# Another queue for the row stores of five segments, and a four-and-two split of the left products, in a recurrent memory transformer with a dense GELU block

## The chip, the cores and the metric

The kernel runs on one core of a Trainium2 chip. The core has five engines with an instruction stream each: TensorE (PE, with its weight loads shown as PEld), VectorE (DVE), ScalarE (ACT), GpSimd (POOL) and SyncE (SP). SP, ACT and POOL issue the transfers (DMA) of this kernel. The metric is the device time of one execution in microseconds (us); lower is better. The time before is the median of three runs.

## The reference

The output is the sum of three things over the same input x of 2048 rows by 1024: x itself, a dense block, and a recurrent attention. Cut to what matters:

```python
xn = layernorm(x)
B = gelu(xn @ w1 + b1) @ w2 + b2                    # 1024 -> 3584 -> 1024
mem = mem0                                          # 8 rows
for s in range(64):                                 # segments of 32 rows
    h = concat([mem, xn[32*s:32*s+32]])             # 40 rows
    q, k, v = h @ Wq, h @ Wk, h @ Wv                # 32 heads of 128
    p = softmax(where(mask, q @ k.T / sqrt(128), -1e9))
    o = (p @ v) @ Wo                                # 40 rows by 1024
    mem, out[s] = o[:8], o[8:]
return x + out + B
```

mask lets every row see the 8 memory rows and the rows up to itself. The loop is a chain: the memory rows of a segment are the first rows of the next one's h. All data is bf16, sums are kept in f32.

## The kernel before

**First stage, up to about 428 us.** Layernorm, the dense block and the residual sum x + B, which is written to DRAM as R_n. The normalised rows go to DRAM too, in the layout that the loop wants (hr_d, hrL_d). While this stage ends, the attention weights are fetched.

**The loop (from L725) over 64 segments, s.** A segment has 64 weight units of 128 x 2048, in the order K0, Q0, K1, Q1, V0, V1 (eight units each, `half_pass`, L767; the digit is the half of the heads) and O (sixteen units, loop at L1104). 46 units live in SBUF. 18 are streamed again from DRAM in every segment into six slots; two of these are kept in PSUM and copied by DVE (L246), one is kept in part. `PLACED` says which units are streamed. As soon as PE has used a streamed unit, `unit_done` (L709) lets SP start the transfer of a later one into its slot, and lets POOL issue one or two entries of a list `small`.

**Main and left rows.** Of each 32 rows a segment handles 24 together with its 8 memory rows (hT, 32 rows, kept in hr_home). The other 8 rows of four segments are gathered into a set of 32 left rows (hL), since nothing in the recurrence waits for them; each half pass of K, Q and V does the left rows once in a group of four segments. i4 is s modulo 4. Where a half pass does both, each weight unit is used twice, by four matmuls each (`product`, L743).

**The turn of the memory rows.** At the end of a segment the sums of O are put together (ACT L1124 where i4 is 1, else DVE L1128), turned by PE (`put_mem`, L295) and copied by DVE into the next hT (L305). Only then can the next K0 begin. Around this stand left products of one of the next segment's half passes, made ahead of time on weights that live in SBUF: up to LEAD = 6, half of them before `put_mem` and the rest behind it:

```python
led.update(next=(w, u, new_acc(), ahead, order), made=0)
lead_products(LEAD // 2)
put_mem(o_sb, nxt["hT"], mixed[:, 224:288], 4 // nw)
if led:
    lead_products(LEAD)
```

They are made at 60 of the 63 turns; in the last group of four segments no next left rows exist.

**Rows out.** The residual rows of a segment are loaded into res_home, which is hr_home[:, 256:512] (for s below 5 by ACT at the start of O, L1075). DVE adds the sums of O to them in place (L1148), and four transfers store 24 rows by 256 columns each to the output (L1182, POOL). Where i4 is 1, the rows go to a DRAM tile first (L1154) and from there to the output by entries of `small` (L1179). The next segment writes the probabilities pdB over res_home[:, 0:128] in `sums(0)` (L915), so that has to wait until the stores have read the rows.

**POOL in the first segments.** For s from 1 to 4, `turn_R` (L438, L467) adds copies of the last residual rows, DRAM to DRAM, to `small`; POOL issues them in order with its other work. `moved_values` (L1097) is a copy of left values on POOL where i4 is 3.

**Order on an engine.** Each engine takes its instructions in the order in which the program lists them. `at` in a segment maps a product's number to functions that are listed behind it: `scores` (PE), `sums` (PE, ACT, DVE), `values` (PE, ACT, DVE), `attend`. PSUM has three accumulator banks (`new_acc`, `let_go`), so a half pass can start only when an earlier one's bank was evicted (`rows_out`, L800).

Of the kernel before, what the change touches and what calls it, by code (L numbers as in the profile page):

```python
# [18 lines left out]
S = 2048  # L19
# [29 lines left out]
SCRATCH = 384  # L49
SMALL = 3712  # L50
LEAD = 6
LATER = 3
LAG = 3
STREAM_BUFS = 6
# [18 lines left out]


ORDER = pass_order()
PLACED = "S..S...." "S...S..." "S....S.." ".S.....S" "....S..." "S..S..S." "...S..S." "S..S..SS"
IS_STREAMED = {unit: PLACED[n] == "S" for n, unit in enumerate(ORDER)}
assert PLACED.count("S") == STREAMED
# [11 lines left out]
def kernel(  # L90
# [142 lines left out]
            fetch(res_tiles[unit], unit)  # L233


    streams = [unit for _ in range(NSEG) for unit in ORDER if IS_STREAMED[unit]]
# [418 lines left out]
    with tc.tile_pool(name="late", bufs=1) as late, \  # L655
# [37 lines left out]
        def unit_tile(unit):  # L693
            nonlocal used
            if IS_STREAMED[unit]:
                place_in_stream[unit] = used
                used += 1
                return stream_tiles.pop(used - 1)[:, :]
            return res_tiles[unit]
# [16 lines left out]
                    if small:  # L716
                        small.popleft()()

        O_UNITS = ORDER[48:]

        hT, hL = nxt["hT"], nxt["hL"]
        kL, VL = [None] * 2, [None] * 2
        led = {}
# [1 line left out]
        for s in range(NSEG):  # L725
# [6 lines left out]


            more = g + 1 < NGRP
            left_k = [first or (i4 == 3 and more), i4 == 0]
            left_q = [first or (i4 == 1 and more), first or (i4 == 2 and more)]
            left_v = [i4 == 0, first or (i4 == 3 and more)]
# [29 lines left out]
            def half_pass(w, u, left, at):  # L767


                ps = new_acc()  # L770
                psL, ahead, order = None, [], list(range(KT))
                if left and led and led["next"][:2] == (w, u):
                    psL, ahead, order = led["next"][2:]
                    assert led["made"] == len(ahead)
                    led.clear()
                elif left:
                    psL = new_acc()
                lag = LAG if first else 0
                tiles = {}
                for n in range(KT + lag):  # L780
                    if n < KT:
                        tiles[n] = unit_tile((w, n, u))
                        product(w, n, tiles[n], hT, ps, range(KT))
                    i = n - lag
                    if i < 0:
                        continue
                    t = tiles.pop(i)
# [6 lines left out]
                    for fn in at.get(i, ()):  # L794
                        fn()
                return ps, psL

# [231 lines left out]
            turn_q(psQ)  # L1029
            if left_q[0] and not first:  # L1030
                turn_qL(psQL, 0)
            psK1, psK1L = half_pass("K", 1, left_k[1], {7: [lambda: scores(0)]})
            exps(0, None if first else lambda: q_left(1))
            st["kT", 1] = nat_home
            rows_out(psK1, nat_home, nc.scalar.copy)
# [1 line left out]
                0: [lambda: nc.vector.transpose(out=nat_home, in_=nat_home)],  # L1037
            }
            if not first:
                at[4] = [lambda: sums(0)]  # L1040
            if left_q[1] and not first:
                at[0].insert(0, lambda: keep_q(1))
            if left_k[1]:
                at[1] = [lambda: turn_kL(psK1L, 1)]
            elif left_k[0]:
                at[1] = [lambda: turn_kL(psKL, 0)]
            psQ1, psQ1L = half_pass("Q", 1, left_q[1], at)
            if first:
                turn_qL(psQ1L, 1)
# [13 lines left out]
                st["V", 0] = values_out(psV, v_home, nc.scalar.copy)  # L1063
                exps(1)

            at = {0: [attend]}
            if left_v[1]:
                at.update({3: [lambda: values(0, (0,))], 5: [lambda: values(0, (1,)), lambda: sums(1)]})
            else:
                at.update({4: [lambda: values(0, (0, 1))], 6: [lambda: sums(1)]})  # L1070

            def load_res():
                st["res"] = res_home
# [22 lines left out]
                VL[1] = late.tile([P, 512], BF16, name="VL1")  # L1096
                nc.gpsimd.tensor_copy(out=VL[1].rearrange("p (h t) -> p h t", t=SEG), in_=ahead_v)  # L1097

            at = {5: [lambda: values(1, (0, 1))]}
            if apart:  # L1100
                at[6] = [moved_values]
# [17 lines left out]
            if not final:  # L1119
                o_sb = outM  # L1120
                no = 16 if left_o else 8
                o = psX[:, 0:32 * no].rearrange("p (h e) -> p h e", e=32)
                if left_o:
                    nc.scalar.copy(out=o_sb[:, 0:no, :], in_=o)  # L1124
                else:
                    o = psX[:, 0:256].rearrange("p (h e) -> p h e", e=16)
                    flat = o_sb.rearrange("p h e -> p (h e)")[:, 0:256].rearrange("p (h e) -> p h e", e=16)
                    nc.vector.tensor_tensor(out=flat, in0=o, in1=st["folded"], op=ALU.add)  # L1128
# [31 lines left out]
            if final:  # L1160
                engines = [nc.sync, nc.scalar]
                n = 0
                for w, r in enumerate(tiles):
                    for b in range(2):
                        cs = slice(256 * (2 * b + w), 256 * (2 * b + w) + 256)
                        pieces = [(rows, slice(64 * b + m0, 64 * b + m0 + NX))]
                        for sl, row in left_rows:
                            p0 = 64 * b + NL * sl
                            pieces.append((slice(row, row + NL), slice(p0, p0 + NL)))
                        for o, i in pieces:  # L1170
                            engines[n % 2].dma_start(out=out_flat[o, cs], in_=r[i, :])
                            n += 1
            elif left_o:
                pairs = [(out_flat[rows, :], outL_d[og, m0:m0 + NX, :])]
                pairs += [
                    (out_flat[row:row + NL, :], outL_d[og, NL * sl:NL * sl + NL, :]) for sl, row in left_rows
                ]
                for o, r in pairs:
                    small.append(lambda o=o, r=r: nc.gpsimd.dma_start(out=o, in_=r))  # L1179
            else:  # L1180
                for j in range(4):
                    nc.gpsimd.dma_start(out=out_flat[rows, 256 * j:256 * j + 256], in_=res[32 * j:32 * j + NX, :])  # L1182
            if not final:
                hT = nxt["hT"]
        while small:
# [34 lines left out]
```

## Time and profile before

| what | value |
|---|---|
| median of three runs | 1843.01 us (1841.55 to 1844.73) |
| the profiled execution | 1840.11 us, of which 1838.4 us between its first and last instruction (the span) |
| PE busy over the span | 1725.6 us, 94% |
| DVE, ACT, POOL busy | 960.6, 668.6, 276.5 us |
| read from and written to HBM | 577.63 MB and 28.97 MB |
| mean granted TensorE clock | 0.995 |

How to read the lines: a row of the timeline has the start in us, the length in us, the engine, the line of the kernel, the operation, the tiles as out<-in, the count, and in brackets how long the engine had been idle and what ended that. A row of the chain of waits has start, length and what the end of the program hung on in that stretch. A row of windows gives the stretch, its length, the busy time of each engine, the granted clock, the DMA engines' busy share and the rate. A row of one line's instructions gives the shortest, median and longest in ns, then the first and last start in us. POOLq, ACTq and SPq are the sequencers of these engines. Matmul ends are modelled and matmuls overlap, so distances between starts say more than lengths.

### The profile page before, as it was taken

Reading aid. Unit: us, or ns where it says so; the run is one execution under the profiler, and the core shown is the slowest. Engines: PE = TensorE matmul, PEld = TensorE weight load, DVE = VectorE, ACT = ScalarE, POOL = GpSimd, SP = SyncE. Lnnn points to the kernel's source line nnn. Section 1 sums busy time; section 2 is a strip of 40 time slices with the busy share of each in tenths; the row PEclk is TensorE's granted clock in tenths of the full one; section 3 lists DMA queues with packets and bytes.
Section 4 is the critical chain, followed back from the end, with each engine's and each line's share of the span. In section 5 each row is a group of like instructions: output and inputs, shape, how many; then the busy total and the mean of one; then the engine's idle time right before and its main releaser. Section 6 shows DMA issues by size and latency. Waiting matters only on the chain.

```text
span 1838.4 us, 71529 instructions
## 1 busy us (share of the span) xinstructions
PE 1725.6 (94%) x31187; PEld 874.2 (48%) x31207; DVE 960.6 (52%) x2443; ACT 668.6 (36%) x1572; POOL 276.5 (15%) x542
## 2 busy tenths in 40 slices
PE   8999999998979999999999899999999999999997
PEld 4444444444444444444444444444545444455443
DVE  7657483705445545455454555545555554545544
ACT  6334251602323333333333333333333343333333
POOL 0000001400341111111121111111111111111111
PEclk9999999999999999999999999999999999999999
DMA  9921212769989999999999999999999999999997
GB/s 289 322 80 46 53 45 58 258 211 362 397 323 381 379 380 374 376 386 370 374 388 362 377 365 393 376 379 375 383 381 392 378 385 368 374 390 390 370 379 305
DMA packets 230599, 596.28 MB, mean 324 GB/s; under 512 B 46539, under 2 KB 86043, under 8 KB 230284
## 3 DMA queue, kind: packets, MB, share of 16 engines
q1 hardware_dynamic: 207028, 571.28, 83.1%
q0 software_dynamic: 16384, 16.64, 2.8%
q8 instruction: 244, 4.00, 0.8%
q10 hardware_dynamic: 6872, 3.78, 0.7%
q14 instruction: 71, 0.58, 0.1%
HBM read 577.63 MB, written 28.97 MB: 330 GB/s over the span
## 4 chain that ended last, share of the span: by engine, by line
PE 66%; DMA 25%; issue 4%; DVE 3%; ACT 2%; POOL 1%; DVEq 0%; ACTq 0%; SPq 0%; POOLq 0%
PE acc L749 30%; PE ps L478 10%; DMA u<-Wc_V 10%; PE acc L984 10%; PE ps L599 8%; DMA u<-Wc_O 6%; DMA u<-Wc_Q 5%; PE ps L632 2%; DMA u<-Wc_K 2%; PE acc L930 2%; DVE d_oL L1005 1%; DVE u L246 1%; DMA hr_home<-hr_d 1%; PE pT L632 1%; DVE q_all L1128 1%
## 5 line engine op out<-in xcount | busy, mean ns | idle before, releaser
L749 PE MATMUL acc<-u,hr_home 128*32 128x512 bf16 x11520 | 791.3, 380 | 40.0 <-DMA u<-Wc_V 18.6
L749 PEld LDWEIGHTS <-hr_home 128*32 128x32 bf16 x12288 | 329.1, 96 | 352.7 <-issue 56.8
L749 PE MATMUL acc<-u,hrL 128*32 128x512 bf16 x2880 | 248.3, 381 | 2.3 <-issue 2.2
L246 DVE TENSOR_SCALAR u<-kept 128x512 uint32<-128x512 uint32 x254 | 163.6, 686 | 70.3 <-PE acc L984 42.1
L478 PE MATMUL ps<-u 128*128 128x512 bf16 (+1 forms) x920 | 195.7, 375 | 2.0 <-ACT u L398 2.0
L800 ACT CAST d_oL<-acc 128x512 bf16<-128x512 f32 x143 | 81.9, 585 | 274.7 <-PE acc L749 274.7
L599 PE MATMUL ps<-u 128*128 128x512 bf16 x657 | 146.2, 379 | 0.8
L984 PE MATMUL acc<-u,q_all 128*32 128x256 bf16 (+1 forms) x2096 | 126.5, 301 | 16.4 <-DMA u<-Wc_O 12.7
L478 PEld LDWEIGHTS <-u 128*128 128x128 bf16 x920 | 90.5, 99 | 105.5 <-issue 2.4
L984 PE MATMUL acc<-u,d_oL 128*32 128x512 bf16 x1944 | 134.3, 383 | 4.6 <-DMA u<-Wc_O 2.0
L1182 POOL DMA_DIRECT2D out_dram<-hr_home x188 | 96.2, 512 | 260.6 <-DVE hr_home L1148 247.8
L814 DVE STREAM_TRANSPOSE q_all<-q_all 128x512 bf16<-128x512 bf16 x128 | 90.7, 708 | 75.4 <-ACT q_all L800 75.3
L984 PEld LDWEIGHTS <-q_all 128*32 128x32 bf16 x3381 | 102.2, 96 | 55.4 <-issue 24.2
L804 ACT CAST q_all<-acc 128x512 bf16<-128x512 f32 x128 | 75.2, 588 | 145.0 <-PE mixed L864 141.0
L911 DVE TENSOR_TENSOR pd_main<-pr_all,mixed 128x320 bf16<-128x320 bf16 x128 | 62.4, 488 | 122.3 <-ACT mixed L902 122.3
L268 POOL DMA_DIRECT2D hr_home<-hr_d x58 | 32.8, 565 | 594.4 <-PE acc L749 594.4
L800 ACT CAST q_all<-acc 128x512 bf16<-128x512 f32 x128 | 75.2, 587 | 98.0 <-PE acc L749 97.8
L749 PEld LDWEIGHTS <-hrL 128*32 128x32 bf16 x3072 | 82.9, 96 | 52.3 <-issue 4.4
L599 PEld LDWEIGHTS <-u 128*128 128x128 bf16 x672 | 65.3, 98 | 77.3 <-DVE g_u L560 0.4
L984 PEld LDWEIGHTS <-d_oL 128*32 128x32 bf16 x2592 | 68.1, 97 | 62.1 <-issue 15.3
L902 ACT ACTIVATE mixed<-mixed,small_consts 128x160 f32<-128x160 f32 x256 | 94.3, 368 | 8.4
L552 ACT ACTIVATE g_xb<-ps,b1col 128x512 bf16<-128x512 f32 x112 | 76.8, 685 | 55.5 <-PE ps L478 54.7
(139 smaller groups left out, 2092.7 us busy)
## 6 DMA issues: line engine op xcount, KB each, us to landing
u<-Wc_K SPq DMA_DIRECT2D x256, 512.0 KB
u<-Wc_V SPq DMA_DIRECT2D x256, 512.0 KB
u<-Wc_O SPq DMA_DIRECT2D x256, 512.0 KB
u<-Wc_Q SPq DMA_DIRECT2D x192, 512.0 KB
u<-in_B_w_dram SPq DMA_DIRECT2D x28, 512.0 KB
hr_home<-hr_d POOLq DMA_DIRECT2D x58, 128.0 KB, 5.3
u<-in_A_Wq_dram SPq DMA_DIRECT2D x13, 512.0 KB
u<-in_A_Wv_dram SPq DMA_DIRECT2D x12, 512.0 KB
```

The source lines that it names most:

```text
L246: nc.vector.tensor_single_scalar(out=out, in_=in_, scalar=0, op=ALU.bitwise_or)
L478: nc.tensor.matmul(ps[:, SEG * s0:SEG * s1].rearrange("p (s t) -> p s t", t=SEG), lhsT=w1_sb[fb // 2][:, kt, (fb % 2) * P:(fb % 2 + 1) * P ...
L552: nc.scalar.activation(out=xb[:, :], in_=ps[:, :], func=ACT.Identity, bias=b1col[:, fb:fb + 1], scale=1.0)
L599: nc.tensor.matmul(ps[:, :], lhsT=gts[fc // 4][:, fc % 4, t * P:(t + 1) * P], rhs=w2_sb[fc // 2][:, fc % 2, cs], start=(fc == 0), stop=(fc ...
L749: nc.tensor.matmul(o, lhsT=lhs[:, i, :], rhs=m, start=(i == seq[0]), stop=(i == seq[-1]), tile_position=(0, 32 * j),)
L800: cp(out=out, in_=ps.rearrange("p (h e) -> p h e", e=32))
L804: cp(out=t[:, :], in_=ps[:, :])
L814: nc.vector.transpose(out=home, in_=home)
L902: nc.scalar.activation(out=mixed[:, 160 * b:160 * b + 160], in_=mixed[:, 0:160], func=ACT.Exp, scale=-1.0, bias=off[:, b:b + 1],)
L911: nc.vector.tensor_tensor(out=pdA.rearrange("p c b q -> p b c q"), in0=prA[:, None, :, :].to_broadcast([P, 2, 4, 40]), in1=dd, op=ALU.mult,)
L984: nc.tensor.matmul(acc[r0:r0 + rows, c:c + wide], lhsT=lhsT, skip_group_check=True, rhs=cols, start=start, stop=stop, tile_position=(0, r0),)
L1182: nc.gpsimd.dma_start(out=out_flat[rows, 256 * j:256 * j + 256], in_=res[32 * j:32 * j + NX, :])
```

## The change

Most of the diff turns constants into tables by i4. With the values given, these say what the code said before: the four strings of PLACED are the old one (so ORDERS[0] to ORDERS[3] are ORDER), scores stand behind product 7, sums(0) behind 4, attend behind 0, values(1) behind 5. Three things differ:

1. The four row stores of a segment go out by ACT's queue where s is below 5 (s = 0, 2, 3 and 4, since s = 1 takes the other branch), and by POOL's from then on.
2. Of the up to six left products made ahead, four stand before `put_mem` and two behind it; three and three before.
3. In the last segment (s = 63) values(0) is done in two halves behind products 3 and 5 of V1, and sums(1) stands behind product 5; before, both halves behind 4, and sums(1) behind 6. All other segments keep their places.

```diff
+LEAD_FIRST = 4
+SCORES_0 = (7, 7, 7, 7)
+SUMS_0 = (4, 4, 4, 4)
+ATTEND = (0, 0, 0, 0)
+VALUES_0 = ((4, 4), (4, 4), (4, 4), (3, 5))
+SUMS_1 = (6, 6, 6, 5)
+VALUES_1 = (5, 5, 5, 5)
...
+def kind_order(placed):
+
+    order = []
+    for n0, n1 in [(n, n + 8) for n in range(0, 64, 8)]:
+        ways = {c: deque(unit for unit in ORDER[n0:n1] if IS_STREAMED[unit] == (c == "S")) for c in "S."}
+        order += [ways[c].popleft() for c in placed[n0:n1]]
+    return order
...
-            at = {0: [attend]}
-            if left_v[1]:
-                at.update({3: [lambda: values(0, (0,))], 5: [lambda: values(0, (1,)), lambda: sums(1)]})
+            at = {0 if first else ATTEND[i4]: [attend]}
+            n0, n1 = (3, 5) if first else VALUES_0[i4]
+            if n0 == n1:
+                at.setdefault(n0, []).append(lambda: values(0, (0, 1)))
             else:
-                at.update({4: [lambda: values(0, (0, 1))], 6: [lambda: sums(1)]})
+                at.setdefault(n0, []).append(lambda: values(0, (0,)))
+                at.setdefault(n1, []).append(lambda: values(0, (1,)))
+            at.setdefault(5 if first else SUMS_1[i4], []).append(lambda: sums(1))
...
-                    order = ahead + [i for i in range(KT) if i not in ahead]
+                    after = [i for w_, i, u_ in ORDERS[(s + 1) % GRP][:48] if (w_, u_) == (w, u)]
+                    order = ahead + [i for i in after if i not in ahead]
                     led.update(next=(w, u, new_acc(), ahead, order), made=0)
-                    lead_products(LEAD // 2)
+                    lead_products(LEAD_FIRST)
                 put_mem(o_sb, nxt["hT"], mixed[:, 224:288], 4 // nw)
...
             else:
+                eng = nc.scalar if s < 5 else nc.gpsimd
                 for j in range(4):
-                    nc.gpsimd.dma_start(out=out_flat[rows, 256 * j:256 * j + 256], in_=res[32 * j:32 * j + NX, :])
+                    eng.dma_start(out=out_flat[rows, 256 * j:256 * j + 256], in_=res[32 * j:32 * j + NX, :])
```

More of the change, by code (lines that the diff above doesn't have):

```diff
@@ L233, in fetch_resident @@
             fetch(res_tiles[unit], unit)
-    streams = [unit for _ in range(NSEG) for unit in ORDER if IS_STREAMED[unit]]
+    streams = [unit for s in range(NSEG) for unit in ORDERS[s % GRP] if IS_STREAMED[unit]]
     late_by = [
@@ L734 @@
             more = g + 1 < NGRP
+            units = ORDERS[i4]
+            O_UNITS = units[48:]
             left_k = [first or (i4 == 3 and more), i4 == 0]
@@ L770, in half_pass @@
                 ps = new_acc()
-                psL, ahead, order = None, [], list(range(KT))
+                now = [i for w_, i, u_ in units[:48] if (w_, u_) == (w, u)]
+                psL, ahead, order = None, [], now
                 if left and led and led["next"][:2] == (w, u):
@@ L781, in half_pass @@
                     if n < KT:
[L782 to L785, printed above, removed]
+                        tiles[now[n]] = unit_tile((w, now[n], u))
+                        product(w, now[n], tiles[now[n]], hT, ps, now)
+                    if n < lag:
                         continue
+                    i = now[n - lag]
                     t = tiles.pop(i)
@@ L793, in half_pass @@
                     unit_done((w, i, u))
-                    for fn in at.get(i, ()):
+                    for fn in at.get(n - lag, ()):
                         fn()
@@ L1031 @@
                 turn_qL(psQL, 0)
-            psK1, psK1L = half_pass("K", 1, left_k[1], {7: [lambda: scores(0)]})
+            psK1, psK1L = half_pass("K", 1, left_k[1], {SCORES_0[i4]: [lambda: scores(0)]})
             exps(0, None if first else lambda: q_left(1))
@@ L1039 @@
             if not first:
-                at[4] = [lambda: sums(0)]
+                at[SUMS_0[i4]] = [lambda: sums(0)]
             if left_q[1] and not first:
```

22 lines of the change are left out of this document (14 added, 8 removed).

## The prediction

> **What bounds the kernel now.** I read the page first (spans, slices, chain), then cut the recurrence, the 64 segments from about 428 us to the end, into windows, and then followed in time order the one segment that stands out.
>
> ```profile
> span 1838.4 us, 71529 instructions
> GB/s 289 322 80 46 53 45 58 258 211 362 397 323 381 379 380 374 376 386 370 374 388 362 377 365 393 376 379 375 383 381 392 378 385 368 374 390 390 370 379 305
> PE 66%; DMA 25%; issue 4%; DVE 3%; ACT 2%; POOL 1%; DVEq 0%; ACTq 0%; SPq 0%; POOLq 0%
> 451.30:494.20 42.90, 40.60 (x904) 21.00 (x900) 22.66 (x58) 15.12 (x39) 15.82 (x29) 1.00 1.02 395
> 494.20:524.70 30.50, 22.20 (x466) 11.15 (x468) 10.94 (x28) 8.60 (x22) 13.27 (x24) 0.89 0.78 279
> 524.70:1810.80 1286.10, 1204.53 (x26822) 626.54 (x26822) 661.01 (x1692) 467.31 (x1208) 203.12 (x386) 1.00 1.00 379
> ```
>
> The windows give length, busy time of PE, PEld, DVE, ACT and POOL, the granted clock, the DMA share and GB/s; I cut them at the copies of the memory rows into the next hT (L305). In the long stretch PE is busy 94% and the DMA engines 100%, so PE and the weight stream are nearly matched: 59 segments take 1286.10 / 59 = 21.80 us each. The slice with 323 GB/s is one segment, s=3, of 30.50 us with the clock at 0.89. It is 30.50 - 21.80 = 8.7 us too long. Its cause:
>
> ```profile
> 496.27 0.29 DVE L1148 TENSOR_TENSOR hr_home<-q_all,hr_home 128x256 bf16<-128x256 bf16 x1 [1.84 <-DMA hr_home<-hr_d]
> 501.23 1.11 POOL L467 DMA_DIRECT2D hr_d<-R_n  x2 [3.40 <-issue]
> 502.87 1.12 POOL L1182 DMA_DIRECT2D out_dram<-hr_home  x2
> 508.37 1.01 POOL L1182 DMA_DIRECT2D out_dram<-hr_home  x2 [4.38 <-issue]
> 503.81 0.49 DVE L911 TENSOR_TENSOR pd_main<-pr_all,mixed 128x320 bf16<-128x320 bf16 x1 [0.29 <-ACT mixed L902]
> 512.33 0.29 DVE L915 TENSOR_TENSOR hr_home<-pr_all,mixed 128x128 bf16<-128x128 bf16 x1 [8.04 <-DMA out_dram<-hr_home]
> 512.54 0.70 DVE L814 STREAM_TRANSPOSE q_all<-q_all 128x512 bf16<-128x512 bf16 x1
> 505.32 0.39 PE L749 MATMUL acc<-u,hrL 128*32 128x512 bf16 x4
> 513.30 0.23 PE L858 MATMUL mixed<-q_all,d_oL 128*32 128x40 bf16 x4 [7.59 <-DVE q_all L814]
> 515.20 0.67 PE L749 MATMUL acc<-u,hr_home 128*32 128x512 bf16 x4
> ```
>
> The rows of s=2 are summed in hr_home by 496.56, but POOL is still working through the residual copies of L467 and issues the four row stores at 502.87 and 508.37. sums(0) of s=3 writes pdB over the same columns (L915), so DVE waits 8.04 us for the stores to have read them; the turn of q stands behind it, then the scores, and PE idles 7.59 us. Afterwards a matmul takes 0.67 us for the usual 0.39, until the clock is back.
>
> **Row stores (s=0, 2, 3, 4; s=1 takes the other branch).** Sixteen DMAs leave POOL's stream and enter ACT's behind the wait for L1148. The 8.7 us goes if the stores of s=2 have read hr_home by the time DVE wants L915, 503.81 + 0.49 = 504.30. Without the wait the turn would end at 504.30 + 0.28 + 0.70 = 505.3 and PE is free only at 505.71, so 0.4 us of lateness is free too. What the new path costs:
>
> ```profile
> L1171 ACTq DMA_DIRECT2D out_dram<-hr_home x3: 303/319/569, 1833.5 to 1834.5; - x3
> L1154 ACTq EVENT_SEMAPHORE  x16: 38/900/1687, 474.6 to 1789.0; - x16
> DMA to landing us min/median/max: 3.3/5.2/6.7
> 540.06 7.16 DMA hr_home<-hr_d
> 497.56 0.58 ACT L800 CAST d_oL<-acc 128x512 bf16<-128x512 f32 x1 [5.48 <-PE acc L749]
> L259 SPq EVENT_SEMAPHORE  x958: 17/17/1283, 321.0 to 1822.0; - x192
> ```
>
> ACT issues a store of this shape in 0.32 us (L1171), four in 1.3 us: 496.6 to 497.9. Landing has no row on ACT for this shape; the bounds are 3.3 us (the best of POOL's own row stores, third line) and 7.16 us (a load issued by ACT in a full stream, fourth line). That ends between 501.2 and 505.1, at worst 0.8 us after 504.30, so 0 to 0.4 us of the stall stays on PE. I take the median, 5.2 us, and nothing left. In s=0, 3 and 4 POOL's stores already arrived in time and nothing is gained.
>
> Behind the stores on ACT stands the eviction of the next K half (L800, 497.56). It comes 497.9 - 497.56 = 0.3 us later. Its two users, the turn on DVE and the accumulator bank for the second K half, come after the Q half of 8 products, 8 x 0.218 = 1.7 us, so the Q half hides it; without that cover it would be 0.3 us in each of four segments. A semaphore wait ahead of each store is the unknown: the ACT rows of L1154, the same kind of store, show 0.04 to 1.69 us. What those waits were for isn't in the row; the transfers issued just before a store (x rows, residual rows, the first K weight) have all landed once L1148 has run and K has begun, so I take 0 of the range 0 to 1.7 us each. SP's weight transfers wait on semaphores in the same way (last row, 0.02 us, at most 1.28), and behind four more transfers a few of them may take the longest; a weight transfer takes some 7 us from issue to landing (870.39 below), so others are under way meanwhile and the stream goes on: 0.
>
> POOL gets lighter by four DMAs in these segments, but loses the stall in which it caught up:
>
> ```profile
> 484.96 1.16 POOL L467 DMA_DIRECT2D hr_d<-R_n  x2
> 520.98 0.61 POOL L1097 COPY VL<-ko 128x512 bf16<-128x512 bf16 x1 [2.27 <-PE acc L936]
> 532.17 0.60 ACT L800 CAST ko<-acc 128x512 bf16<-128x512 f32 x1
> ```
>
> Thirteen copies ran from 484.96 to 502.87, 17.9 us. The next thirteen would then end near 521 and put L1097 there. The next writer of those ko columns is ACT's eviction at about 532.2 - 8.7 = 523.5, so 0, and at most 1 us of ACT if POOL is slower than that.
>
> On the stream's side the same stall is worth much the same: at 279 GB/s the 30.50 us moved 8.51 MB, which at the 395 GB/s of the two segments before takes 21.5 us (9.0 saved), at 379 GB/s 22.5 us (8.0). **Term: -8.7 us, from -7.6 (with 0.4 left on PE and the slow rate) to -9.1.**
>
> **Four left products, then two, for 60 of the 63 turns of the memory rows.** A long run of products, one turn as it is, and one of the three turns that have no left products:
>
> ```profile
> 496.68 4.32 PE L749 MATMUL acc<-u,hr_home 128*32 128x512 bf16 x76
> 764.15 0.83 PE L749 MATMUL acc<-low,hrL 128*32 128x512 bf16 x12
> 764.73 0.42 DVE L1128 TENSOR_TENSOR q_all<-acc,d_oL 128x256 bf16<-128x256 f32 x1
> 765.21 0.21 PE L295 MATMUL mixed<-ident_mem,q_all 128*128 128x32 bf16 x2 [0.23 <-DVE q_all L1128]
> 765.36 0.83 PE L749 MATMUL acc<-u,hrL 128*32 128x512 bf16 x12
> 766.02 0.39 PE L749 MATMUL acc<-u,hr_home 128*32 128x512 bf16 x4
> 1766.78 0.22 PE L295 MATMUL mixed<-ident_mem,q_all 128*128 128x32 bf16 x2 [0.88 <-DVE q_all L1128]
> 1767.32 0.40 PE L749 MATMUL acc<-u,hr_home 128*32 128x512 bf16 x4 [0.32 <-DVE hr_home L305]
> ```
>
> A product is four matmuls side by side; 76 of them are 19 products, whose starts lie (4.32 - 0.40) / 18 = 0.218 us apart. Three begun at 764.15 leave PE's input free at 764.15 + 3 x 0.218 = 764.80; the turn starts at 765.21, because DVE's sum ends at 765.15. A fourth fits into that 0.41 us whole. Behind the turn K starts 766.02 - 765.21 = 0.81 us later; one product less makes it 0.59, and the rows without products show that hT is ready 1767.32 - 1766.78 = 0.54 us after the turn. So PE gains 0.218 us a turn, with 0.05 us to spare; 60 x 0.218 = 13.1 us if PE alone set the pace. If hT were later than those three rows show, up to 0.05 x 60 = 3 us of it would go back.
>
> It doesn't set it alone. Three readings bound what comes through:
>
> ```profile
> 764.73 0.44 DVE q_all L1128
> 765.43 1.61 PE acc L749 x25
> 870.39 7.09 DMA u<-Wc_Q
> 640.00:650.00 10.00, 9.94 (x255) 4.99 (x247) 4.99 (x15) 5.24 (x14) 0.56 (x1) 1.00 1.02 404
> 651.00:660.00 9.00, 8.91 (x167) 4.46 (x170) 4.41 (x10) 1.17 (x2) 1.45 (x3) 1.00 0.88 298
> 1572.60:1638.30 65.70, 60.94 (x1367) 32.04 (x1370) 34.07 (x87) 23.23 (x60) 9.87 (x19) 1.00 1.00 383
> 1745.30:1810.80 65.50, 58.02 (x1286) 29.81 (x1278) 31.36 (x82) 23.15 (x60) 9.87 (x19) 1.00 1.00 382
> ```
>
> The chain of waits passes through the turn (first two lines, the turn at 765) at 42 of the 60; at 18 it runs past it inside a transfer, mostly a weight (third line, over the turn at 873.9). So at most 42 x 0.218 = 9.2 us. Around a turn the stream sometimes runs below its rate (0.88 and 298 GB/s against 1.02 and 404), since few weight slots are free; there an earlier K frees a slot earlier and the gain goes through. Against it: the last three turns' segments (1745.30 to 1810.80) have 60.94 - 58.02 = 2.9 us less PE work than the same three of an earlier group, and are only 0.2 us shorter, at the same GB/s. That is 0.07 of the work taken away. Between 0.07 and 42/60 = 0.7 I take 0.3, nearer to the measured pair than to the chain, since a chain moves to another path as soon as it is shortened. **Term: 0.3 x 13.1 = -3.9 us, from -0.9 to -9.2.**
>
> **The rest.** The four orders are equal to the old one, and the placing of scores, sums and values is the old one for all but the last segment, where values(0) is split around two products and sums(1) comes one product earlier: one product either way, 0, from -0.2 to +0.3 us.
>
> **Sum.** -8.7 - 3.9 = -12.6 us. On the profiled execution (1840.11 us, with 1838.4 of span and 1.7 around it) that gives 1827.5; the median shown is 2.9 us higher, so 1843.0 - 12.6 = 1830.4 for the median.
>
> **Rivals.**
> *The stream alone sets the pace.* DMA share 1.00 and the pair of 65.70 and 65.50 speak for it, the rates near the turns against. Only the stall goes: -8.7 - 0.9 = -9.6, 1833.4 us.
> *PE sets it.* The chain speaks for it, the pair against. -8.7 - 9.2 = -17.9, 1825 us; with all 13.1, 1821.
> *The stall stays, with another engine's name.* The stores would have to reach hr_home as late as now. This is what the Trainium skill, DMA: Bandwidth & Descriptors, section Issuing engines are not separate DMA queues, would make one expect: transfers of all issuing engines run on the same 16 DMA engines, and another issuer saves only the time to issue. The trace sets that time at nearly the whole: the last store was issued 509.38 - 496.56 = 12.8 us after its rows were ready, and had read them 3 us later. With a landing as long as it would take, 504.3 + 8 - 497.9 = 14 us against at most 7.16 seen, the stall stays and only the split is left, 1839 us, or 1842 with 0.07 of it.
> *Slower: ACT blocks.* The stores stand ahead of the K eviction. If each waits 1.69 us on a semaphore (the longest row of L1154), the eviction comes 4 x 1.69 + 0.3 = 7 us late, 1.7 of it covered; PE loses 5.3 us in four segments, 21 us, against 12.6 gained: 1851 us. It decides from 12.6 / 4 + 1.7 = 4.9 us of lateness per segment. Against it: ACT's rows hold short waits where the transfers ahead are old.
>
> **Chances.** Forecast 0.42 (1827 to 1833), stream alone 0.28, PE 0.15, stall stays 0.08, slower 0.07. The range takes in the first three with both terms at their ends and 2 us of scatter of a median: 1820 to 1838; outside lie the last two, 0.15. A measurement here tells 0.2%, 3.7 us, from nothing. Faster by more: the first three and half of the fourth, 0.89; within: the other half, 0.04; slower: 0.07.
>
> **What would show it.** After the change no DVE wait of L915 on row stores above 1 us, no window below 350 GB/s in the recurrence and no clock below 0.98 near 510; sixteen L1182 rows on ACT's queue of 0.3 us each; L800 after them at most 0.5 us later; the products ahead of and behind a turn as x16 and x8, K 0.59 us after L295. Wrong would be: a wait of K1 for its bank, K waiting for L305 in most turns, or a median above 1838.

## The result, and the profile after

| | before | after |
|---|---|---|
| median beside each other on one chip, 20 runs each | 1842.28 us | 1834.47 us |
| ratio, 95% interval | | 0.9958 [0.9944, 0.9972] |
| profiled execution, its span | 1840.11, 1838.4 us | 1831.03, 1828.9 us |
| mean granted TensorE clock | 0.995 | 0.999 |

The change makes the kernel faster by 0.42%: 0.0042 x 1842.28 = 7.7 us (5.2 to 10.3). The forecast was 12.6 us less. Lines of the changed kernel lie some 25 to 31 lower: L915 is now L941, L1148 is L1178, L1182 is L1213, L467 is L492, L1097 is L1126, L800 is L826, L749 is L774, L295 is L320, L305 is L330, L1128 is L1157.

The windows of the kernel after, cut at the same copies into hT as before:

```profile
450.20:493.83 43.63, 40.55 (x898) 20.56 (x890) 22.34 (x58) 15.16 (x39) 12.68 (x24) 1.00 1.02 383
493.83:517.28 23.45, 21.45 (x476) 11.25 (x472) 10.88 (x29) 8.56 (x22) 7.81 (x15) 1.00 1.01 384
517.28:1807.50 1290.22, 1207.82 (x26935) 628.51 (x26935) 663.55 (x1698) 469.65 (x1210) 204.08 (x386) 1.00 1.00 380
```

The stretch of s=3 is 23.45 us instead of 30.50, its clock is 1.00 and its rate 384 GB/s. The timeline of that stretch and of the next one's start shows why:

```profile
495.85 0.29 DVE L1178 TENSOR_TENSOR hr_home<-q_all,hr_home 128x256 bf16<-128x256 bf16 x1 [1.43 <-DMA hr_home<-hr_d]
...
496.17 1.58 ACTq L1213 DMA_DIRECT2D out_dram<-hr_home  x4
496.24 0.55 POOL L492 DMA_DIRECT2D hrL_d<-R_n  x1 [2.34 <-issue]
...
497.79 0.59 ACT L826 CAST d_oL<-acc 128x512 bf16<-128x512 f32 x1 [5.75 <-PE acc L774]
...
504.22 0.28 DVE L941 TENSOR_TENSOR hr_home<-pr_all,mixed 128x128 bf16<-128x128 bf16 x1
...
519.71 0.62 POOL L1126 COPY VL<-ko 128x512 bf16<-128x512 bf16 x1
```

The stores begin to leave 0.3 us after the sum of the rows has begun, while POOL is still at the residual copies, and the next segment writes pdB over the rows (L941) at 504.22. In the view of L941 alone none of its instructions has an idle time before it, and its longest is 289 ns:

```profile
L1213 ACTq DMA_DIRECT2D out_dram<-hr_home x16: 319/374/598, 451.6 to 542.5; - x16
L1213 ACTq EVENT_SEMAPHORE  x4: 38/3855/4047, 447.3 to 536.8; - x4
...
L941 DVE TENSOR_TENSOR hr_home<-pr_all,mixed x64: 280/280/289, 435.6 to 1810.6; 128x128 bf16<-128x128 bf16 x64
```

The traces hold no landing time for a store that ACT issued. One of the turns, and the idle times by what ended them, of the kernel after, for the other half of the change:

```profile
448.92 1.05 PE L774 MATMUL acc<-u,hrL 128*32 128x512 bf16 x16
449.90 0.21 PE L320 MATMUL mixed<-ident_mem,q_all 128*128 128x32 bf16 x2
450.04 0.61 PE L774 MATMUL acc<-u,hrL 128*32 128x512 bf16 x8
450.49 0.39 PE L774 MATMUL acc<-u,hr_home 128*32 128x512 bf16 x4
```
```profile
PEld L774 <- DVE hr_home L330: 19.4, 63, 1.2
PE acc L774 <- DVE hr_home L330: 2.2, 5, 0.7
PE mixed L320 <- DVE q_all L1157: 1.8, 2, 0.9
PE acc L774 <- DMA u<-Wc_V: 24.7, 56, 1.8
PE acc L774 <- DMA u<-Wc_Q: 11.6, 19, 1.7
PE acc L774 <- DMA u<-Wc_K: 4.3, 7, 1.7
```

A row of this second view names the waiting engine and line, what it waited for, the sum in us, how often, and the longest. The same view of the kernel before:

```profile
PE mixed L295 <- DVE q_all L1128: 10.1, 38, 0.9
PE acc L749 <- DMA u<-Wc_V: 18.6, 45, 1.8
PE acc L749 <- DMA u<-Wc_Q: 10.0, 16, 1.2
PE acc L749 <- DMA u<-Wc_K: 1.6, 5, 0.6
```

Four products are ahead of the turn and two behind it, and K starts 450.49 - 449.90 = 0.59 us after it, as reckoned. PE's wait for the sums of O fell from 10.1 to 1.8 us; its waits for weights of V, Q and K rose from 18.6 + 10.0 + 1.6 = 30.2 to 24.7 + 11.6 + 4.3 = 40.6 us. So in these two profiles what PE saved at the turn comes back as longer waits for weights; more profiles of the same kernels, below, don't all show it.

### The profile page after: what moved, and what is told of

It reads as the page before. It is cut to its first block, busy times and chain, and to the rows that moved or that the text cites. A ratio compares the mean times of both kernels' runs of the same rounds, so it can differ in the third digit from the quotient of the medians.

```text
span 1828.9 us, 71537 instructions
## 1 busy us (share of the span) xinstructions
PE 1723.1 (94%) x31207; PEld 873.1 (48%) x31207; DVE 959.5 (52%) x2443; ACT 670.1 (37%) x1572; POOL 269.3 (15%) x526
## 4 chain that ended last, share of the span: by engine, by line
PE 65%; DMA 30%; issue 2%; DVE 1%; ACT 1%; SPq 0%; ACTq 0%; POOL 0%; DVEq 0%; POOLq 0%
PE acc L774 29%; DMA u<-Wc_V 13%; PE ps L503 11%; PE acc L1010 10%; PE ps L624 8%; DMA u<-Wc_O 7%; DMA u<-Wc_Q 5%; DMA u<-Wc_K 3%; PE ps L657 2%; PE acc L956 2%; DMA hr_home<-hr_d 1%; DVE u L271 1%; PE pT L657 1%; PE mixed L320 0%; PE mixed L884 0%
## 5 line engine op out<-in xcount | busy, mean ns | idle before, releaser
L774 PE MATMUL acc<-u,hr_home 128*32 128x512 bf16 x11520 | 793.4, 380 | 52.7 <-DMA u<-Wc_V 24.7
L774 PEld LDWEIGHTS <-hr_home 128*32 128x32 bf16 x12288 | 327.9, 96 | 374.5 <-issue 70.2
L774 PE MATMUL acc<-u,hrL 128*32 128x512 bf16 x2880 | 250.4, 380 | 1.7 <-issue 1.5
L826 ACT CAST d_oL<-acc 128x512 bf16<-128x512 f32 x143 | 82.0, 586 | 270.5 <-PE acc L774 258.4
L1213 POOL DMA_DIRECT2D out_dram<-hr_home x172 | 88.1, 512 | 243.1 <-DVE hr_home L1178 237.7
L826 ACT CAST q_all<-acc 128x512 bf16<-128x512 f32 x128 | 75.3, 589 | 93.4 <-PE acc L774 93.4
L774 PEld LDWEIGHTS <-hrL 128*32 128x32 bf16 x3072 | 83.4, 96 | 48.1 <-issue 2.8
```

The lines of the kernel that those rows point to most:

```text
L774: nc.tensor.matmul(o, lhsT=lhs[:, i, :], rhs=m, start=(i == seq[0]), stop=(i == seq[-1]), tile_position=(0, 32 * j),)
L826: cp(out=out, in_=ps.rearrange("p (h e) -> p h e", e=32))
L1213: eng.dma_start(out=out_flat[rows, 256 * j:256 * j + 256], in_=res[32 * j:32 * j + NX, :])
```

## The experiments

There are twelve runs of ten kernels, in three groups, each group on one chip beside the kernel before (whose medians there were 1840.2, 1839.35 and 1840.22 us). Ratios are to it. Line numbers below are those of before, unless said. Theory A is the prediction's: the stall goes through the row stores, the split is worth some of its 13.1 us.

**One part alone.** stores_only takes the row stores to ACT and leaves the split at three and three:

```diff
+                eng = nc.scalar if s < 5 else nc.gpsimd
                 for j in range(4):
-                    nc.gpsimd.dma_start(out=out_flat[rows, ...
+                    eng.dma_start(out=out_flat[rows, ...
```

> The kernel before with the row stores of s = 0, 2, 3 and 4 on ACT's queue, and left products three and three as before. Theory A (the wait of s = 3 is nearly all of the gain): its segment of 30.5 us comes down to 22 to 24 us, DVE's L915 waits for no row store, and the time falls by 6 to 9 us of 1842. Theory B (the wait is made up later, because it leaves all six weight slots full, and the split made the gain): the segment gets shorter, the following ones get longer by about as much, and the time falls by 0 to 3 us.

split_only leaves the stores on POOL:

```diff
-                    lead_products(LEAD // 2)
+                    lead_products(4)
```

> The kernel before with four left products ahead of the turn and two behind it; row stores on POOL's queue as before. Theory A (the weight stream takes up what the turns give): K begins 0.22 us earlier behind the turns, PE's waits for weights grow by 6 to 11 us in total, the time falls by 1 to 4 us and the wait of 8 us in s = 3 stays. Theory B (PE sets the pace at two turns of three): waits for weights grow by less than 4 us, and the time falls by 7 to 10 us.

stores_only: 1836.92 us, ratio 0.9967 [0.9951, 0.9983], so -6.1 us (-9.0 to -3.1); no wait for the stores, and the stretch of s=3 is 22.08 us. split_only: 1839.41 us, ratio 0.9998 [0.9977, 1.0019], so -0.4 us (-4.2 to +3.5); the stretch of s=3 is 30.25 us. Its waits:

```profile
DVE hr_home L915 <- DMA out_dram<-hr_home: 8.6, 1, 8.6
PE mixed L858 <- DVE q_all L814: 8.0, 1, 8.0
...
PE mixed L295 <- DVE q_all L1128: 1.8, 2, 0.9
```

The stall of 8.6 us stays and the turn is as short as after the change: the parts act separately, and the split alone could not be told from nothing. PE's waits for weights of V, Q and K didn't grow here (15.0 + 10.8 + 2.3 = 28.1 us against 30.2), so theory A was nearer on the time and wrong on the waits, and theory B the other way round.

**The stores of s=2 alone.** Only those had shown a wait. If the sentence of the prediction is right that s=0, 3 and 4 gain nothing, moving these is enough.

```diff
+                eng = nc.scalar if s == 2 else nc.gpsimd
```

> The kernel before with the row stores of s = 2 alone on ACT's queue; those of s = 0, 3 and 4 stay on POOL's. Theory A (only the stores of s = 2 were late): the same time as stores_only within 2.5 us, segment 3 without a wait for row stores. Rival (the stall moves to the next segment whose stores stand behind POOL's copies, s = 3 or 4, since POOL no longer catches up in the stall): a wait of 3 to 8 us for row stores at L915 of s = 4 or 5, and 3 us or more above stores_only.

1839.74 us, ratio 0.9999 [0.9981, 1.0016]: nothing is left of the gain. The waits, then POOL in time order:

```profile
DVE hr_home L915 <- DMA out_dram<-hr_home: 6.9, 1, 6.9
```
```profile
520.79 0.55 POOL L467 DMA_DIRECT2D hrL_d<-R_n  x1
521.34 0.62 POOL L1097 COPY VL<-ko 128x512 bf16<-128x512 bf16 x1
521.89 0.55 POOL L1183 DMA_DIRECT2D out_dram<-hr_home  x1
...
525.66 1.00 POOL L1183 DMA_DIRECT2D out_dram<-hr_home  x2 [2.12 <-issue]
```

(L1183 is the row store here.) The stretch of s=3 is 21.55 us, that of the next segment 27.49: the stall of 6.9 us has moved by one segment. In the kernel before, the stores of s=3 were in time only because POOL had caught up during the stall. So moving the stores of s=2 alone isn't enough; s=0 and s=4 were not tried by themselves.

**The cause on the other side: fewer copies in the queue.** copies_spread leaves the stores on POOL and spreads the residual copies of turn_R over s=1 to 8, half as many in each.

```diff
-        def turn_R(ttg, eng, small=None):
+        def turn_R(ttg, eng, small=None, segs=range(4)):
...
-            for i in range(4):
+            for i in segs:
...
-            if 1 <= s <= 4:
-                turn_R(NT - 5 + s, nc.gpsimd, small)
+            if 1 <= s <= 8:
+                turn_R(NT - 4 + (s - 1) // 2, nc.gpsimd, small, range(2 - s % 2 * 2, 4 - s % 2 * 2))
```

> The kernel before, row stores on POOL's queue, three and three, but the residual copies of four segments of POOL's list are given out over eight, half as many in each. Theory A (POOL's copies, 13 or more in a segment, make it late with the stores): no wait for row stores at L915 above 1 us, segment 3 at 21 to 24 us, and the time as stores_only's, 4 to 9 us below before. Rival (the row stores are slow by themselves on POOL's queue, or the wait moves to a later segment): a wait of over 3 us at L915 stays in one of s = 3 to 9, and the time is within 3 us of before.

1839.71 us, ratio 0.9991 [0.9973, 1.0009]: the time is the one that the rival expected. The stretch of s=3 is 21.06 us without a wait for stores, so the copies ahead of the stores were the cause. But the stretch of s=6, which ends with the copy at 584.8 us, is 27.25 us long. POOL in that stretch, then the wait in the view of all waits:

```profile
568.21 1.16 POOL L467 DMA_DIRECT2D hr_d<-R_n  x2
...
574.38 1.12 POOL L467 DMA_DIRECT2D hr_d<-R_n  x2 [2.40 <-issue]
575.50 0.55 POOL L467 DMA_DIRECT2D hrL_d<-R_n  x1
579.53 0.59 POOL L268 DMA_DIRECT2D hr_home<-hr_d  x1 [3.48 <-issue]
```
```profile
DVE hr_home L305 <- DMA hr_home<-hr_d: 9.2, 5, 6.6
```

From s=5 on POOL also issues the load of the segment's x rows (L268), and here it comes behind the copies; the hT copy waits 6.6 us for it. The copies delay whatever stands behind them.

**The split the other way.** lead_0_6 has the stores on ACT and all six left products behind the turn.

```diff
-                    lead_products(LEAD // 2)
+                    lead_products(0)
```

> Row stores on ACT's queue, and all six left products behind the turn of the memory rows, none ahead of it. Against three and three PE loses 3 x 0.218 = 0.65 us in each of 60 turns, 39 us. Theory A (the stream sets the pace, PE has about 1 us a segment to spare): the time is 0 to 20 us above that of stores_only, and PE's waits for weights shrink by what PE lost beyond that. Theory B (PE sets the pace): it is 30 to 39 us above stores_only.

1848.79 us, ratio 1.0043 [1.0024, 1.0062]; against stores_only of the same group +11.9 us by the medians. From the turn to K it takes 1.46 us on the mean of the segments from s=5, against 0.83 in stores_only: 0.63 x 60 = 38 us more on PE, of which 11.9 / 38 = 0.3 arrives in the time. Its waits:

```profile
PE mixed L295 <- DVE q_all L1128: 39.9, 47, 0.9
...
PE acc L749 <- DMA u<-Wc_V: 17.5, 38, 1.8
...
PE acc L749 <- DMA u<-Wc_Q: 1.2, 3, 0.7
```

The same waits of stores_only:

```profile
PE acc L749 <- DMA u<-Wc_V: 22.9, 57, 2.1
...
PE acc L749 <- DMA u<-Wc_Q: 9.8, 14, 1.6
```

While K starts later the weights arrive, and PE waits 5.4 + 8.6 = 14 us less for those of V and Q: so a longer turn is in part paid back by shorter waits for weights.

**With less of a stream.** light_3_3 and light_4_2 have the stores on ACT and differ in the split. V's four streamed units are not streamed; the tile of the next resident unit is used in their place.

```diff
+SKIPPED = [unit for unit in ORDER if unit[0] == "V" and IS_STREAMED[unit]]
+IS_STREAMED.update((unit, False) for unit in SKIPPED)
...
+            if unit in SKIPPED:
+                return res_tiles[unit[0], unit[1] + 1, unit[2]]
             return res_tiles[unit]
```

> Row stores on ACT's queue, three and three, and the four streamed units of V are not streamed: their products take the next unit of V that lives in SBUF (the output is another one for that). Twelve transfers of a weight in a segment for sixteen, PE's work unchanged. Theory A (the weight stream is what takes up PE's gains): PE's waits for weights fall from 49 us to under 12 us, DMA share falls to about 0.8, and the time falls by 40 to 70 us. Theory B (PE sets the pace already): the time falls by less than 25 us.

> The same lighter stream with four and two. Theory A: with weights always there the split pays in full, 10 to 13 us below light_3_3, though with the whole stream it paid 0 to 4. Rival (the turn is not PE's to shorten: K waits for hT or for its weights' loads whatever stands ahead of it): 0 to 4 us here too.

light_3_3: 1772.1 us (1764.86 to 1774.69), ratio 0.9615 [0.959, 0.964]. light_4_2: 1765.35 us (1764.2 to 1771.81), ratio 0.9596 [0.9572, 0.9619]. By the ratios the split is worth 0.0019 x 1839 = 3.5 us, by the medians 6.7, and the intervals overlap. The two profiled spans are 1770.0 and 1769.7 us, but light_4_2's profiled run (1771.81) was the slowest of its four; the others took 1764.2 to 1765.58. One window over both, 500 to 1700 us, first three and three, then four and two:

```profile
500.00:1700.00 1200.00, 1151.90 (x26138) 614.48 (x26130) 644.23 (x1648) 456.45 (x1180) 200.18 (x378) 1.00 0.83 294
```
```profile
500.00:1700.00 1200.00, 1153.69 (x26152) 616.23 (x26149) 643.28 (x1647) 456.61 (x1180) 198.43 (x375) 1.00 0.82 294
```

With the DMA engines 17% free PE should have been the bound and 13 us the gain; they don't come in these profiles. From s=5 on the turn takes 0.598 us instead of 0.814, yet the mean segment 20.94 instead of 20.93. PE's waits show most of where it goes, first light_3_3, then light_4_2 (L753, L297 and L1132 are L749, L295 and L1128):

```profile
PE mixed L297 <- DVE q_all L1132: 12.3, 47, 0.9
...
PE acc L753 <- issue: 7.4, 13, 1.2
```
```profile
PE acc L753 <- issue: 12.4, 13, 1.7
...
PE mixed L297 <- DVE q_all L1132: 1.8, 2, 0.9
```

Over all lines of PE, between the copy into hT that begins s=5 and the last one, the idle time put down to issue is 17.6 and 27.6 us, 10.0 more, while the waits for weights fall from 8.7 to 7.1. These idles are about 1 us long, and each of those over 0.5 us (15 and 24 of them) ends 1.1 to 1.8 us after a packet of 16 KB has ended on the DMA queue that the page calls instruction; of moments drawn at random 0.12 have such a packet there. So PE seems to wait for its own instructions. Their sum differs between executions of one kernel: 17.7, 19.5 and 26.9 us in the three profiles of the changed kernel. That the two spans are alike is therefore in good part chance.

A smaller part stands at streamed units. In the 14 segments with i4 = 0 from s=8 on, in the mean distances between the starts of products on hr_home (0.22 us is one product):

```
K0 last to Q0 first   light_3_3 0.22   light_4_2 0.31
K1 fifth to sixth     light_3_3 0.25   light_4_2 0.40
end of Q1, light_4_2 less light_3_3: +0.29 us, counted from K0's first start
```

Q0's first and K1's first and sixth are streamed units. The longer distances stand in seven places of light_4_2 and one of light_3_3, and make some 3.5 us in all. This led to theory E: the transfers of the next few streamed units are started by slots that come free during O, ahead of the turn, so they come no earlier when the turn is shorter. Theory R, its rival: the stream's rate as a whole takes the gain.

**Other units left out.** early_3_3 and early_4_2 are the same pair, but V's units are streamed, and the five streamed units that come first behind a turn are not (K0's two, Q0's first, K1's two; Q0's fifth is kept in PSUM as before).

```diff
+SKIPPED = [unit for unit in ORDER if IS_STREAMED[unit] and unit != IN_PSUM and (unit[0] == "K" or unit == ("Q", 0, 0))]
```

> Row stores by ACT, split three and three; the five streamed units that come first after a turn (K0's two, Q0's first, K1's two) are not streamed: the next resident unit's tile is used in their place, so the output is another and 28% of the weight stream (5 of 18 units) is gone. The units of O, V and Q1 are streamed as before. Both theories: PE sets the pace, 1760 to 1785 us, as in light_3_3 (1772.1). It is the base for early_4_2.

> As early_3_3, with the split four and two. Theory E (the split's 0.218 us a turn is lost at the first streamed units behind the turn, whose transfers were started before the turn and do not come earlier when the turn is shorter): here no such unit is left, so 60 x 0.218 = 10 to 13 us less than early_3_3, and the segment sums from s=5 on fall by about 0.2 us. Theory R (the rate of the stream as a whole, or something in PE's own order, takes it): 0 to 7 us less, as in the pair light_3_3 and light_4_2, with segment sums that stay within 0.08 us.

early_3_3: 1778.14 us (1773.72 to 1779.56), ratio 0.9662 [0.9638, 0.9685]. early_4_2: 1765.25 us (1763.58 to 1765.87), ratio 0.9594 [0.9569, 0.9618]. The split is worth 12.9 us by the medians, and no run of one lies within the runs of the other. The spans differ by 1777.6 - 1763.3 = 14.3 us, and the mean segment from s=5 on by 20.958 - 20.744 = 0.21 us, all of it at the turn (0.816 and 0.598). First the groups of products and the wait ahead of the turn of early_3_3, then those of early_4_2:

```profile
L753 PE MATMUL acc<-u,hr_home 128*32 128x512 bf16 x11008 | 713.8, 380 | 0.6 <-issue 0.6
...
PE mixed L297 <- DVE q_all L1132: 58.3, 46, 2.0
```
```profile
L753 PE MATMUL acc<-u,hr_home 128*32 128x512 bf16 x11008 | 713.2, 380 | 0.1
...
PE mixed L297 <- DVE q_all L1132: 47.1, 45, 2.0
```

Products on streamed weights wait for nothing here (0.6 and 0.1 us in the last field, where light_3_3 has 19.1 and the kernel after 52.7), and of the 11.2 us by which the wait ahead of the turn falls nothing comes back as a wait for weights. The DMA share is 0.82 and 0.83 over the same window as above, as in the light pair: so the load of the DMA engines as a whole, theory R, isn't the difference. The split pays in full where no streamed unit stands close behind the turn, as theory E expected. But this pair differs from the light one in two more things. PE waits 58.3 and 47.1 us for the sums of O instead of 12.3 and 1.8, so the chain through the turn sets its pace at most turns; and its idle time put down to issue is 1 us instead of 18 and 28. No run separates the three, so theory E isn't shown to be the reason in the light pair or in the kernel as it is.

**The pair once more as it is.** stores_again and after_third are stores_only and the changed kernel, side by side; after_again is the changed kernel in the second group.

> The same as stores_only (row stores by ACT, split three and three), run again beside after_third to size the split in the kernel as it is. Prediction on record: after_third is 3.9 us lower than this one. Theory E and theory R both: 0 to 2 us lower; stores_only itself some 6 to 8 us below before.

> The changed kernel once more on the same chip. Prediction on record: 3.9 us below stores_again. Theories E and R: 0 to 2 us below it.

> The changed kernel once more, on the chip of the three others. Theory A: 6 to 10 us below before, and 0 to 4 us below stores_only's ratio of 0.9967, that is 0.9945 to 0.9967. Theory B (PE sets the pace at most turns): 0.991 to 0.993.

after_again: 1832.42 us, ratio 0.9942 [0.9921, 0.9964], between the ranges that theories A and B had for it. after_third: 1830.61 us, ratio 0.9963 [0.9943, 0.9983]. stores_again: 1836.42 us, ratio 0.9987 [0.9967, 1.0007]. Between the last two the split is worth 0.0024 x 1840 = 4.4 us, with an interval of some 5 to either side; with split_only's 0.4 that gives two readings, both between 0 and 5. The 4.4 are nearer to the 3.9 on record than to the 0 to 2 that theories E and R expected, but the interval takes in all of them. The stores alone show 6.1 and 2.4 us in the two groups, where 6 to 8 were expected of the second. Single runs of one kernel lie up to 20 us apart here, so the two terms stay known to 3 to 5 us each; their sum is the better known, 7.7, 10.7 and 6.8 us in three groups.

## Why the prediction came out as it did

**Sign and mechanism: right.** The row stores on ACT took the stall away; undone alone (split_only) it is back, done in part (store_s2) it moves. The time of 1834.47 us lies in the range, 4 us above the forecast of 1830.4, and nearest to the rival in which the stream alone sets the pace (1833.4).

**The stall's term, -8.7 us: too large.** The lengths of the stretches from one hT copy to the next, in the profiles of before and split_only, which have the stall, and of after and the four more that have all stores of the first segments on ACT at four and two or three and three:

```
              s=1    s=2    s=3    s=4    s=5    sum
before        22.35  20.59  30.50  22.59  22.10  118.1
after         23.44  20.60  23.45  21.90  23.87  113.3
split_only    22.07  20.15  30.25  21.82  23.37  117.7
stores_only   23.08  20.97  22.08  22.64  23.38  112.2
stores_again  22.40  21.08  22.08  23.30  22.92  111.8
after_third   23.16  21.32  21.89  22.67  22.80  111.8
after_again   22.57  20.52  21.59  22.46  23.04  110.2
```

From before to the mean of the five, the stretch itself falls from 30.50 to 22.2, 8.3 us: that is the term. But the two behind it grow from 44.7 to 45.8 and the two ahead from 42.9 to 43.8, so that 6.3 of it is left. split_only has 45.2 behind and 42.2 ahead, and one of the five profiles differs from another by up to 1.4 us there, so these growths are known to about 1 us. The step that failed is "It is 30.50 - 21.80 = 8.7 us too long": it takes the stall's price from one stretch and holds its neighbours fixed. The stream's own reckoning, "the 30.50 us moved 8.51 MB", failed in the same way: after the change that stretch moved 23.45 us x 384 GB/s = 9.00 MB. During a stall transfers still under way fill the weight slots, and PE has them at hand in the segments behind it; with the stall this goes too. That account fits the two stretches behind; it was argued from the bytes and not tried by itself. For the two ahead the traces name a path. The stretch of s=1 is 22.4 to 23.4 us in these five, with the stores of s=0 on ACT, and 22.0 to 22.4 in the four with them on POOL (before, split_only, store_s2, copies_spread); PE's waits for weights of V in it are 0.5 to 1.2 us and 0 to 0.3. So some 0.8 us goes with the new path of these stores, which the prediction had at 0. How the stores on ACT delay those weights stays open. (The end of -9.1 in the term's range has no working there; the stream's reckoning gives 9.0.)

**The split's term, 0.3 x 13.1 = -3.9 us: its 0.22 us a turn was exact, the share that comes through is small and known poorly.** In the two tries it is 0.4 and 4.4 us of 13.1, so 0.03 and 0.34; neither rules out the 0.3. The step "Between 0.07 and 0.7 I take 0.3, nearer to the measured pair than to the chain" leaned the right way, and lead_0_6 gives 0.3 for a lengthening. The upper bound, "So at most 42 x 0.218 = 9.2 us", was no price that could be reached: after the change the chain still runs through 41 of the 60 turns, while at most half of those 9.2 us were seen in the two tries. That an earlier K frees a slot earlier "and the gain goes through" is not borne out: only in the early pair, without streamed units close behind the turn, do all 13 us arrive. What takes the rest in the kernel as it is stays open. Two things that scatter by as much as the gain stand in the way: PE's waits for weights of V, Q and K are 30.8, 35.1 and 40.6 us in the three profiles of the changed kernel and 36.0 and 36.2 in the two with the stores alone, and the idle time put down to issue in these five is 14.0 to 26.9 us from s=5 on.

**"In s=0, 3 and 4 POOL's stores already arrived in time and nothing is gained": wrong for s=3, without harm to the sum.** It reads the trace of before as if the stall weren't part of it. store_s2 shows the stall going over to s=3.

**The stall stays, with another engine's name: ruled out.** The Trainium skill, DMA: Bandwidth & Descriptors, section Issuing engines are not separate DMA queues, was weighed there: another issuer saves only the time to issue. No run here shows the landing of a store from ACT. ACT's last store of s=2 was issued by 497.75 and L941 began at 504.22 without a wait, so the rows were read within 6.5 us of it, inside the 3.3 to 7.16 us that the prediction allowed; POOL's own row stores land in 5.2 us in the median before and after. So nothing here speaks against the rule, but the time to issue was the whole stall.

**Slower, ACT blocks: no, but the lateness was put too low, and its cover was thin.** A store takes 374 ns in the median rather than 0.32 us, and a group of four 1.58 to 1.78. For s=2 the K eviction follows at once, at 497.79, and the Q eviction comes 1.67 us behind it, against 1.81 before; so K's is about 0.1 us late. For s=3:

```profile
519.88 1.58 ACTq L1213 DMA_DIRECT2D out_dram<-hr_home  x4
521.50 0.59 ACT L826 CAST d_oL<-acc 128x512 bf16<-128x512 f32 x1 [7.33 <-PE acc L774]
522.25 0.59 ACT L826 CAST q_all<-acc 128x512 bf16<-128x512 f32 x1 [0.16 <-PE acc L774]
```

There K's eviction starts 521.50 - 517.91 = 3.59 us behind K's first product, against 527.22 - 525.27 = 1.95 before. So it was 1.6 us late, three times the 0.5 that the prediction allowed as a sign; in the other four profiles with these stores on ACT it was 0 once and 1.6 to 2.1 us else. The rows' sum on DVE came later against K than in s=2, since it waited for the load of the residual rows. The Q half of 1.7 us just covered it: no PE wait in that stretch is on an eviction. In stores_again it did not: the eviction was 2.0 us late, and the second K half waited 0.7 us for it, a sign that the prediction had named as wrong.

Of semaphore waits ahead of the stores, priced at 0 of 0 to 1.7 us each, the kernel after has one for each group of four, 3.9 us in the median. In three of the four groups it ends as the load of the residual rows lands (451.2, 519.0 and 540.9), which ACT itself had issued and the rows' sum needs as well; most of it is time that ACT had free. None stands between the stores of a group there. In stores_only and stores_again one store of the group of s=3 took 1.1 and 1.2 us, and the traces don't say why.

**The rest.** L1126 starts at 519.71 for "near 521"; the last segment's tail is 27.3 us for 27.6. K waits for the hT copy in every turn, as its weight load shows (19.4 us in 63 turns, 0.31 each), but PE's matmuls only in 5 (2.2 us). So the sign "K waiting for L305 in most turns" came for the weight loads and not for the matmuls: the margin of 0.05 us was as narrow as computed, and with a third product moved ahead K would most likely have waited for hT instead.

## What to carry to other kernels

A wait on a small store can be a wait on what stands ahead of it in its issuing queue. Look at the transfers of that kind that come next, too: moving only the one that waits handed the stall to the next. Price a stall over its neighbours and not by its own stretch alone. A saving on an engine that shares the bound with a stream can arrive in small part only, however many times the chain of waits passes there: here 0.4 and 4.4 of 13 us with the whole stream, and 12.9 where no streamed operand stood close behind it. And one profile of each kernel doesn't say where a few us went, when executions of one kernel differ by 9 us in PE's idle time put down to issue alone.

## What was not expected of the hardware

GpSimd's queue fell behind by far more than its own instructions take. In the kernel after, its copies take 0.55 to 0.59 us each, yet they come in groups with idle times of 2 to 4 us between, which the timeline puts down to issue:

```profile
498.84 1.13 POOL L492 DMA_DIRECT2D hr_d<-R_n  x2 [2.05 <-issue]
...
504.10 1.11 POOL L492 DMA_DIRECT2D hr_d<-R_n  x2 [3.58 <-issue]
...
510.42 0.55 POOL L492 DMA_DIRECT2D hrL_d<-R_n  x1 [4.12 <-issue]
```

The landing times in the trace show what ends them. The copy issued at 498.84 landed at 503.75, and the next group began at 504.10; the one issued at 504.10 landed at 510.09, and the next began at 510.42. All 18 such idles over 0.3 us between 440 and 640 us end within 0.35 us after POOL's oldest transfer under way has landed, with two to six under way until then; in the kernel before it is all 15. So POOL's queue seems to wait for its own transfers, of some 5 us each, once a few are under way. That explains the 12.8 us by which it was late; what sets the number wasn't tried. ScalarE's queue took groups of four such stores in 1.58 to 1.78 us in the kernel after, in the same full stream, without such a gap; it was never given more than four at a time.

PE, too, had idle times that no change here touched: 14 to 28 us of issue in the loop of all the kernels but the early pair, the larger ones each just behind a packet of the instruction queue, as shown at the light pair.
